# Sliding-window attention, one head to a slot: two complementary triangles merged in PSUM by a predicated copy, exponentiated once, parted on Pool

## Chip, cores, metric

One core of one Trainium2 chip. The metric is the device time in microseconds (us) of one execution. A kernel's time is the median of its runs. The runs e1 to e8 were made on one chip and e9 to e12 on another, each beside before on the same chip. TensorE is called PE, VectorE DVE, ScalarE ACT, GpSimd Pool. "Low clock" means the stretches in which the profile shows PE's granted clock at one half; the clock given for a run is the mean over its span, 1 being full speed.

## The reference, cut to what matters

```python
# A: full attention, B: sliding window; both: S=2048, D=512, H=32 heads of Dh=16
# x, wqkv, wo: bf16, normal * 0.05
scores = einsum("bhqd,bhkd->bhqk", q, k) * (Dh ** -0.5)
# B only, with W = 256:
mask = (idx[:, None] - idx[None, :] >= 0) & (idx[:, None] - idx[None, :] < W)
scores = where(mask, scores, -1e9)
p = softmax(scores);  o = einsum("bhqk,bhkd->bhqd", p, v);  out = o @ wo
# result: concatenate([A, B], axis=-1)
```

In B a block of 128 queries sees three blocks of 128 keys: its *own*, of which it may use the triangle key <= query; the *middle* one, whole; and the *far* one, of which it may use the triangle key > query. The two triangles are complementary: laid over each other they fill one 128x128 block exactly. The change rests on that.

## The kernel before

A *slot* is a PSUM tile of three parts of 512 fp32 columns, called banks here: PE writes scores (keys on the partitions, queries on the columns), ACT takes the exponential of all 1536 columns in one instruction, PE multiplies the result with V some slots later. There are two score buffers, so the scores of slot s+2 can only start when the exponential of slot s is done. Everything else (projections, masks, output) is put in between as fill.

A head has 16 dimensions and a guard row, so its score matmul is issued on 32 rows (32\*128 in the trace, where a matmul over all rows is 128\*128). Four heads of a group sit on four row groups (`tile_position=(32 * jb.j, 0)`). A slot takes three consecutive jobs, so its matmuls use three different row groups. In front of them goes a matmul over all 128 rows whose result is overwritten. It is called the warming matmul because of what it does to the granted clock: without it in window slots the clock was 0.861 in place of before's 0.939 (e3 below).

```python
def scores(self, slot):                     # before
    sps = self.ps.tile([P, SLOT, 512], FP32, name="sps", tag="sps", bufs=2)
    for b, jb in enumerate(slot["jobs"]):
        r = slice(32 * jb.j, 32 * jb.j + KR)
        ...
        if b == 0 and self.filled < 2:      # the warming matmul, full AND window slots
            kT, k0 = self.kT[jb.inst, jb.g // 2, jb.subs[0][0] // 4]
            self.nc.tensor.matmul(sps[:, 0, 0:WARM], lhsT=kT[:, gg, k0:k0 + P],
                                  rhs=qT[:, gg, 0:WARM], start=True, stop=True)
        for kt, q0, q1, o in jb.subs:
            ...
            self.nc.tensor.matmul(sps[:, b, o:o + q1 - q0], lhsT=kT[r, gg, k0:k0 + P],
                                  rhs=qT[r, gg, q0:q1], start=True, stop=True,
                                  tile_position=(32 * jb.j, 0))

# run(), cut: per slot
self.exps(sl)
if s + 2 < len(slots):
    self.scores(slots[s + 2])
self.values(s - 1 - any(j.inst for j in sl["jobs"]))
# ... then fill work
```

A window head of before is 3 x 512 columns: own, middle and far blocks are all exponentiated, then DVE multiplies the own triangles by a mask (`tensor_mul`, line 491) and Pool zeroes the far ones (`affine_select`, line 493).

## Time and profile before

| | before |
|---|---|
| time, median of 4 runs | 1170.76 us (1166.48 to 1172.31) |
| span of the profiled run, mean granted clock | 1169.9 us, 0.939 |
| ACT busy / PE busy | 94% / 79% |
| time at the low clock | 145 us in 21 periods |

The prediction below shows the engines' busy line, the groups and a steady stretch of the timeline. Three more lines matter here. The first is from the page's second part, the granted clock in 40 equal slices, in tenths of full speed; then the largest wait of ACT (who waits <- for whom: us in all, times, longest); then the stretch from 300 to 500 us (PE, PE weight load, DVE, ACT, Pool busy, granted clock, DMA share, GB/s).

```profile
PEclk9999899998999898999999999999999999976777
```
```profile
ACT pT L480 <- PE sps L462: 31.1, 64, 2.1
```

### The profile page before, as it was taken

Reading aid. Unit: us, or ns where it says so; the run is one execution under the profiler, and the core shown is the slowest. Engines: PE = TensorE matmul, PEld = TensorE weight load, DVE = VectorE, ACT = ScalarE, POOL = GpSimd, SP = SyncE. Lnnn points to the kernel's source line nnn. Section 1 sums busy time; section 2 is a strip of 40 time slices with the busy share of each in tenths; the row PEclk is TensorE's granted clock in tenths of the full one; section 3 lists DMA queues with packets and bytes.
Section 4 is the critical chain, followed back from the end, with each engine's and each line's share of the span. In section 5 each row is a group of like instructions: output and inputs, shape, how many; then the busy total and the mean of one; then the engine's idle time right before and its main releaser. Section 6 shows DMA issues by size and latency. Waiting matters only on the chain.

```text
span 1169.9 us, 17451 instructions
## 1 busy us (share of the span) xinstructions
PE 926.1 (79%) x6844; PEld 270.6 (23%) x6944; DVE 298.2 (25%) x674; ACT 1098.6 (94%) x841; POOL 119.0 (10%) x316
## 2 busy tenths in 40 slices
PE   6788888878878887777778787787777887788893
PEld 3222222222222222222222222222222222222221
DVE  3442121132123222222322232224223132320101
ACT  3789999998999999999999999999999999999992
POOL 4000000010001001011200121102112011210100
PEclk9999899998999898999999999999999999976777
DMA  6022421221222112211220221124012112210101
GB/s 207 10 77 75 99 83 41 61 63 52 65 78 76 45 42 65 70 47 61 83 66 32 75 76 54 39 68 118 26 48 65 65 65 69 66 43 18 57 19 55
DMA packets 72810, 73.87 MB, mean 63 GB/s; under 512 B 22688, under 2 KB 55832, under 8 KB 72728
## 3 DMA queue, kind: packets, MB, share of 16 engines
q1 hardware_dynamic: 69656, 68.83, 19.3%
q10 hardware_dynamic: 2432, 1.84, 0.5%
q0 software_dynamic: 640, 2.10, 0.5%
q8 instruction: 54, 0.88, 0.3%
q14 instruction: 28, 0.23, 0.1%
HBM read 39.06 MB, written 31.58 MB: 60 GB/s over the span
## 4 chain that ended last, share of the span: by engine, by line
ACT 62%; PE 21%; issue 11%; DVE 3%; DMA 1%; POOL 0%; ACTq 0%; another core or an unknown queue 0%; SPq 0%; DVEq 0%; POOLq 0%
ACT pT L480 61%; PE sps L462 6%; PE sps L457 6%; PE ms L202 4%; PE op L514 4%; DVE va L285 1%; DVE osb L533 1%; PE ms L591 0%; DMA den<-od 0%; DVE pT L491 0%; DMA rb<-rd 0%; PE sps L358 0%; ACT xT L610 0%; DVE padmax L394 0%; DVE kTa L392 0%
## 5 line engine op out<-in xcount | busy, mean ns | idle before, releaser
L480 ACT ACTIVATE pT<-sps 128x1536 bf16<-128x1536 f32 (+4 forms) x827 | 1088.4, 1566 | 32.8 <-PE sps L462 31.1
L457 PE MATMUL sps<-qTa,kTa 128*128 128x512 bf16 x659 | 261.0, 396 | 159.2 <-ACT pT L480 152.9
L462 PE MATMUL sps<-qTa,kTa 32*128 32x512 bf16 x2048 | 286.5, 404 | 1.5 <-ACT pT L480 1.5
L514 PE MATMUL op<-pT,va 128*32 128x512 bf16 x2048 | 216.4, 412 | 0.5 <-DVE osb L533 0.3
L493 POOL TENSOR_SCALAR_AFFINE_SELECT pT<-pT 128x256 bf16<-128x256 bf16 (+2 forms) x224 | 102.5, 475 | 967.7 <-issue 556.6
L462 PEld LDWEIGHTS <-kTa 32*128 32x128 bf16 x2048 | 68.2, 91 | 395.3 <-issue 395.3
L491 DVE TENSOR_TENSOR pT<-pT,mlo 128x256 bf16<-128x256 bf16 (+2 forms) x256 | 74.9, 334 | 136.3 <-ACT pT L480 134.9
L457 PEld LDWEIGHTS <-kTa 128*128 128x128 bf16 x659 | 64.3, 98 | 144.4 <-issue 124.4
L514 PEld LDWEIGHTS <-va 128*32 128x32 bf16 x2048 | 53.7, 94 | 125.5 <-issue 125.0
L457 PE MATMUL sps<-qTb,kTb 128*128 128x512 bf16 x128 | 51.2, 400 | 34.8 <-ACT pT L480 32.7
L533 DVE COPY osb<-op 128x512 f32<-128x512 f32 x64 | 44.2, 691 | 85.2 <-PE op L514 84.9
L462 PE MATMUL sps<-qTb,kTb 32*128 32x384 bf16 (+2 forms) x704 | 58.4, 289 | 0.0
L220 DVE CAST kst<-ms 128x512 bf16<-128x512 f32 x28 | 19.4, 691 | 141.4 <-PE ms L202 141.4
L343 DVE CAST ob<-ms 128x512 bf16<-128x512 f32 x28 | 19.4, 691 | 131.8 <-PE ms L202 131.8
L301 DVE CAST qs<-ms 128x512 bf16<-128x512 f32 x31 | 21.4, 690 | 115.1 <-PE ms L202 115.1
L514 PE MATMUL op<-pT,vb 128*32 128x384 bf16 (+2 forms) x704 | 36.6, 290 | 0.9 <-DVE osb L533 0.7
L202 PE MATMUL ms<-xT,wq 128*128 128x512 bf16 x91 | 32.2, 408 | 4.7 <-issue 4.3
L462 PEld LDWEIGHTS <-kTb 32*128 32x128 bf16 x704 | 16.9, 93 | 79.7 <-issue 79.7
L202 PE MATMUL ms<-wv,xT 128*128 128x512 bf16 x103 | 32.0, 398 | 4.2 <-issue 1.6
L202 PE MATMUL ms<-xT,wk 128*128 128x512 bf16 x89 | 30.9, 413 | 3.5 <-issue 2.7
L285 DVE CAST vb<-ms 128x512 bf16<-128x512 f32 x16 | 11.1, 692 | 84.5 <-PE ms L202 84.5
L312 DVE CAST gs<-ms 8x512 bf16<-8x512 f32 x31 | 21.0, 677 | 20.0 <-PE ms L310 20.0
(80 smaller groups left out, 274.8 us busy)
## 6 DMA issues: line engine op xcount, KB each, us to landing
od<-osb SPq DMA_DIRECT2D x64, 256.0 KB
oc<-od SPq DMA_DIRECT2D x32, 256.0 KB
rb<-rd SPq DMA_DIRECT2D x32, 256.0 KB
kTb<-kd SPq DMA_DIRECT2D x16, 256.0 KB
qTb<-qd SPq DMA_DIRECT2D x16, 256.0 KB
qd<-qs SPq DMA_DIRECT2D x31, 128.0 KB
qTa<-qd SPq DMA_DIRECT2D x15, 256.0 KB
out_dram<-ob SPq DMA_DIRECT2D x30, 128.0 KB
```

What stands on the lines that cost most here:

```text
L202: self.nc.tensor.matmul(bank, lhsT=lhs(c), rhs=rhs(c), start=(c == 0), stop=(c == NC - 1))
L220: copy(out=kst[:], in_=bank)
L285: copy(out=v3[:, :, 1:VP], in_=bank.rearrange("p (h d) -> p h d", d=DH))
L301: copy(out=qs[:], in_=bank)
L312: self.nc.vector.tensor_copy(out=gs[:], in_=b[0:8, :])
L457: self.nc.tensor.matmul(sps[:, 0, 0:WARM], lhsT=kT[:, gg, k0:k0 + P], rhs=qT[:, gg, 0:WARM], start=True, stop=True)
L462: self.nc.tensor.matmul(sps[:, b, o:o + q1 - q0], lhsT=kT[r, gg, k0:k0 + P], rhs=qT[r, gg, q0:q1], start=True, stop=True, tile_position=(3 ...
L480: nc.scalar.activation(out=pT[:, b:e, :n], in_=sps[:, b:e, :n], func=ACT.Exp, scale=SCALE)
L491: nc.vector.tensor_mul(out=v, in0=v, in1=self.mlo[:, 0:e - b, :])
L493: nc.gpsimd.affine_select(v, v, pattern=[[0, e - b], [-1, P]], compare_op=ALU.is_ge, fill=0.0, base=-1, channel_multiplier=1)
L514: self.nc.tensor.matmul(op[32 * jb.j:32 * jb.j + 32, q0:q1], lhsT=self.v[jb.inst, kt][:, h * VP:h * VP + 32], rhs=slot["pT"][:, b, o:o + q ...
L533: nc.vector.tensor_copy(out=osb[:], in_=self.op[i, p, g][:])
```

## The change

Intent: take exponentials away from ACT, which sets the time. A window slot becomes one head. Its nine score matmuls fill own and middle blocks (1024 columns) and, behind them, the far blocks (512 columns). DVE copies the far triangles over the forbidden halves of the own blocks, PSUM to PSUM, by a predicated copy. ACT then exponentiates 1024 columns in place of 1536, and Pool parts the triangles afterwards.

```diff
 def scores(self, slot):
+    jb = slot["jobs"][0]
+    if i == 1:                                   # a window slot: one head, no warming matmul
+        r = slice(32 * jb.j, 32 * jb.j + KR)
+        for kt, q0, q1, o in jb.near + jb.far:
+            ...
+            self.nc.tensor.matmul(sps[:, o:o + q1 - q0], lhsT=kT[r, gg, k0:k0 + P],
+                                  rhs=qT[r, gg, q0:q1], start=True, stop=True,
+                                  tile_position=(32 * jb.j, 0))
+        m = jb.blocks(sps[:], "merged")
+        ...
+        self.nc.vector.copy_predicated(m, mask.broadcast_to(tuple(m.shape)),
+                                       jb.blocks(sps[:], "last"))
+        return
+    if self.filled < 2:                          # warming matmul: full slots only
         ...
 def exps(self, slot):
+    nc.scalar.activation(out=pT[:, :n], in_=sps[:, :n], func=ACT.Exp, scale=SCALE)
-            for kind, o in jobs[b].blocks:
-                if kind == "d":
-                    nc.vector.tensor_mul(out=v, in0=v, in1=self.mlo[:, 0:e - b, :])
-                else:
-                    nc.gpsimd.affine_select(...)
+            nc.gpsimd.affine_select(jb.blocks(pT[:], "last"), m, ...)   # far triangle out
+            m = jb.blocks(pT[:], "own")
+            nc.gpsimd.affine_select(m, m, ...)                          # own triangle stays
 def slots(self):                                 # heads spread between the full slots
+            for m, h in enumerate(flat):
+                extra.append((a0 + 2.5 + m * (a1 - a0 - 6) / len(flat), h))
 # cut: classes _Job and _Window, values() by groups, smaller rings of buffers
```

## The prediction

> **What bounds the kernel now.** I read the page's first and second parts, then the groups with shapes kept apart, then the timeline around a few slots, then the waits.

> ```profile
> PE 926.1 (79%) x6844; PEld 270.6 (23%) x6944; DVE 298.2 (25%) x674; ACT 1098.6 (94%) x841; POOL 119.0 (10%) x316
> ```
> ScalarE is busy 94% of the span, nearly all of it (1088.4 us on the page) in the exponentials of line 480. PE at 79% comes second and is not far off.

> ```profile
> L480 ACT ACTIVATE pT<-sps 128x1536 bf16<-128x1536 f32 x782 | 1058.6, 1608 | 30.4 <-PE sps L462 28.9 <-DVE pT L491 1.0
> L480 ACT ACTIVATE pT<-sps 128x1024 bf16<-128x1024 f32 x9 | 9.6, 1091 | 0.0
> L480 ACT ACTIVATE pT<-sps 128x768 bf16<-128x768 f32 x10 | 8.6, 918 | 0.0
> ...
> L491 DVE TENSOR_TENSOR pT<-pT,mlo 128x384 bf16<-128x384 bf16 x86 | 30.9, 381 | 77.1 <-ACT pT L480 76.3 <-POOL pT L493 0.7
> ...
> L493 POOL TENSOR_SCALAR_AFFINE_SELECT pT<-pT 128x384 bf16<-128x384 bf16 x70 | 43.2, 625 | 265.7 <-issue 177.9 <-ACT pT L480 79.7 <-POOL pT L493 4.4
> ```
> The mean of 1608 ns is not what an exponential costs: 782 of them in 1058.6 us is 1.35 us each, because neighbours overlap. The masks on VectorE and Pool wait for ScalarE; nothing on ScalarE waits for them but 1.0 us. So taking masks off VectorE is worth nothing by itself.

> ```profile
> 403.98 0.38 PE L457 MATMUL sps<-qTa,kTa 128*128 128x512 bf16 x1 [0.31 <-ACT pT L480]
> 404.28 0.10 PEld L462 LDWEIGHTS <-kTa 32*128 32x128 bf16 x3 [0.59 <-issue]
> 404.29 0.39 PE L462 MATMUL sps<-qTa,kTa 32*128 32x512 bf16 x3
> 404.61 0.10 PEld L514 LDWEIGHTS <-va 128*32 128x32 bf16 x4 [0.23 <-issue]
> 404.61 0.40 PE L514 MATMUL op<-pT,va 128*32 128x512 bf16 x4
> 404.94 0.10 PEld L457 LDWEIGHTS <-kTa 128*128 128x128 bf16 x1 [0.23 <-issue]
> 405.32 0.38 PE L457 MATMUL sps<-qTa,kTa 128*128 128x512 bf16 x1 [0.31 <-ACT pT L480]
> ```
> This is the steady rhythm. PE waits until the exponential of slot s has freed one of the two score buffers, runs a warming matmul, the three score matmuls of slot s+2 at once, and values. The next release comes 1.34 us later: that is the true price of one 1536-column exponential. The scores are complete 0.70 us after the release, so they are ready 0.6 us early.

> **The cost of an exponential.** The trace has exponentials starting 1.330 us apart for 1536 columns and 0.904 us for 1024, which is 0.83 ns a column; taking 1.343 us for 1536 from the matmuls' releases, 1024 cost 0.917, 896 cost 0.810, 512 cost 0.490. The 782 large ones then need 1050.2 us and the 45 small ones 29.3, together 1079.5. From the first exponential's start to the last one's end the trace shows 1121.2 us, so 41.7 us are stalls. About 15 us of idling lie before 100 us (projections of the full instance crowd PE) and about 9 after 1000 us (PE on the lowered clock). In the middle are some 15 stalls of 1.1 to 1.2 us where the granted clock halves for a moment (matmuls of 0.38 us turn into 0.62), and about 9 us at window units with uneven slots.

> [...] A stalled exponential pays more: the one at 1026.29 us, that had waited for PE, took 1.45 us, which is 0.17 over its columns. [...] the three score matmuls of a slot, on three row groups, start 3 ns apart.

> **The change, part by part.** *Removed on ScalarE.* In the built program the list of exponentials has 682 of 1536 columns and one of 1024 (the full instance), 96 of 1024 and 32 of 896 (the window, a head each). That is 682 x 1.343 + 97 x 0.917 + 32 x 0.810 = 915.9 + 88.9 + 25.9 = 1030.8 us, against 1079.5: **48.7 us less** on the path that sets the end, mostly because a head exponentiates 1024 columns in place of 1536.

> *Added ahead of the exponential.* A window slot now holds one head, so its nine score matmuls (1536 columns) all use one row group and run in series; then VectorE merges 4 x 128 columns from PSUM to PSUM; only then may ScalarE start. From the release of the buffer at time 0: 0.03 to PE's start; 1536 columns at 2.4 per ns (512-column projection matmuls start 0.215 us apart) with about 3 ns between matmuls (the startup transposes of 128 columns, each with new weights, are 56 ns apart) = 0.67, and the last one's pipeline 0.16, so 0.86; 0.05 to VectorE (a PE end at 428.62 and its copy at 428.67); the merge, taken as the 0.69 of the 512-column PSUM copy; 0.06 to ScalarE. So the input is ready at 1.69, and the exponential, no longer overlapped, ends 0.17 + 0.85 later, at 2.71. Undisturbed, it would end at 1.343 + 0.917 = 2.26. **A stall of about 0.44 us for each of 96 heads, 42 us.** The 32 heads of the first quarter have six matmuls of 1152 columns and merge 256 (0.42): 0.03 + 0.69 + 0.05 + 0.42 + 0.06 + 0.93 = 2.18 against 2.15, about 1 us in all. VectorE is busy 19% of the time with other things than masks ((298.2 - 74.9) / 1170), half of one being 0.35 us: up to 0.07 us each if waits fall at random, and since many of its operations come before the merge's turn I count 3 us for all 128.

> *Moved.* The 256 mask products (75 us) leave VectorE and 128 merges come (96 x 0.69 + 32 x 0.42 = 80 us): even. Pool gets 256 selects, the most of 512 columns; from 334, 468 and 625 ns for 128, 256 and 384 columns I extrapolate 0.77 us, so about 180 us in place of 104. Window values are now issued after the full unit's, slots later, so this is hidden. Those values come as one burst of 36 matmuls, about 0.75 us of PE: the following slots catch up, and PE has gained some slack since window slots run no warming matmul.

> *Returned.* The uneven window slots of before (about 9 us of stalls) are gone. Startup's filler is 40 x 128 columns in place of 24 x 256 and no longer waits for the padding selector: at most 1 us.

> Sum: 1171 - 48.7 + 42 + 1 + 3 - 9 - 1 = **1158 us**.

> **The rivals.** (1) *The merge is hidden and ScalarE's saving comes through whole*: then 1171 - 48.7 - 5 is about 1117. For it: VectorE is idle 75% of the time, and the merge waits for no other slot. Against it: the 0.6 us of slack that scores have now is smaller than 0.69 + 0.3 of added chain, and two score buffers forbid an earlier start. (2) *The chain is longer than I think*: [...] (3) *The clock.* When ScalarE waits for VectorE, PE waits too[...]. At half clock the window's scores take 1.3 us and its stall grows to about 1.1: with a third of window slots so, +20 us, 1180.

> **Range and chances.** The gain on ScalarE is arithmetic. What I don't know is the chain of 96 slots, where 0.1 us is 10 us of the time; a chain shorter by 0.25 us gives 1134, one longer by 0.3 gives 1187. So 1125 to 1190 eight times in ten. Faster by over 2% needs under 1147.6, a chain about 0.11 us shorter than mine or fewer clock drops: 0.34. Slower needs over 1194.5, rival 2 in full: 0.12. The rest, 0.54, within 2%.

> **What would show it.** The page after should show ScalarE busy near 1050, at a share near 91%, and a wait of its exponentials for VectorE's merge of some 40 us that before doesn't have; merges of 0.69 and 0.42 us; nine window scores spaced as their columns. If that wait is small, rival 1 holds; if merges last 1.2 us, or the nine take over 1 us, rival 2; if the granted clock is lower than 0.939 with window scores of double length, rival 3. I am wrong on the whole if ScalarE stalls somewhere else: at the bursts of window values, or behind VectorE work that waits for a transfer (its reciprocals waited 55.5 us for transfers in all), since the merges now queue behind it.

## More of the kernel before

```profile
300.00:500.00 200.00, 159.98 (x1189) 45.59 (x1207) 52.61 (x121) 194.28 (x159) 17.51 (x44) 0.96 0.20 61
```

Each of the four slices with an 8 holds 6.8 to 10.2 us at half speed. ACT hardly waits: 31 us for PE in the whole kernel, and it is busy 194 of the 200 us.

## The result, and the profile after

| | before | after |
|---|---|---|
| time, median of 4 runs | 1170.76 us | 1254.65 us (1250.15 to 1258.31) |
| ratio to before, 95% interval | | 1.0721 (1.0667 to 1.0775) |
| mean granted clock of the profiled run | 0.939 | 0.817 |
| time at the low clock (periods) | 145 us (21) | 462 us (41) |

A ratio is always the mean time of one kernel's fast runs over that of the other's in the same rounds, so it is not quite the ratio of the medians. Executions over 1.5% slower than the fastest of the same kernel are left out of the means. The change made the kernel 7.2% slower, and the prediction's range does not hold it.

The page's busy line and granted clock:

```profile
PE 1045.6 (83%) x7436; PEld 348.2 (28%) x7536; DVE 308.6 (25%) x545; ACT 1072.0 (85%) x825; POOL 172.0 (14%) x348
...
PEclk8998978679999866977898788869865989676667
```

ACT does less work, as intended, but is busy for only 85% of a longer span. PE is busy 120 us more although its warming matmuls before window slots are gone. The second line says why: many slices have 6, 7 or 8.

Groups of ACT and DVE with shapes kept apart (busy us, mean ns of one | idle just before them, and what ended it):

```profile
L484 ACT ACTIVATE pT<-sps 128x1536 bf16<-128x1536 f32 x682 | 943.5, 1472 | 55.1 <-PE sps L470 52.1
L484 ACT ACTIVATE pB<-sps 128x1024 bf16<-128x1024 f32 x96 | 98.3, 1024 | 82.5 <-DVE sps L456 67.6 <-PE op L523 14.0 <-DVE den L558 0.9
L484 ACT ACTIVATE pB<-sps 128x896 bf16<-128x896 f32 x32 | 29.4, 917 | 9.2 <-DVE sps L456 5.4 <-PE op L523 3.8
```
```profile
L456 DVE COPY_PREDICATED sps<-after,sps 128x512 f32<-128x512 int8 x96 | 66.8, 696 | 262.8 <-PE sps L449 221.1 <-ACT pT L484 28.5 <-issue 12.8
L456 DVE COPY_PREDICATED sps<-after,sps 128x256 f32<-128x256 int8 x32 | 13.7, 429 | 85.2 <-PE sps L449 82.2 <-issue 3.0
```

The shapes and counts are those predicted, and so is the price of a merge. The idle time before window exponentials is 92 us in all, 73 of it for the merge. In the timeline at full clock (start, duration, engine, what, idle before) the chain looks like this:

```profile
443.13 0.82 PE L449 MATMUL sps<-qTb,kTb 32*128 32x256 bf16 x9 [0.25 <-ACT pT L484]
...
444.05 0.70 DVE L456 COPY_PREDICATED sps<-after,sps 128x512 f32<-128x512 int8 x1 [0.43 <-PE sps L449]
...
444.84 1.02 ACT L484 ACTIVATE pB<-sps 128x1024 bf16<-128x1024 f32 x1 [0.42 <-DVE sps L456]
```

Nine matmuls in 0.82 us, 0.10 to DVE, a merge of 0.70, 0.09 to ACT: 1.71 us from PE's start to ACT's. And at half clock:

```profile
489.28 1.45 ACT L484 ACTIVATE pT<-sps 128x1536 bf16<-128x1536 f32 x1 [0.18 <-PE sps L470]
489.66 0.61 PE L462 MATMUL sps<-qTa,kTa 128*128 128x512 bf16 x1
490.20 0.61 PE L470 MATMUL sps<-qTa,kTa 32*128 32x512 bf16 x3
...
491.71 1.46 PE L449 MATMUL sps<-qTb,kTb 32*128 32x256 bf16 x9
...
493.27 0.70 DVE L456 COPY_PREDICATED sps<-after,sps 128x512 f32<-128x512 int8 x1
```

The nine matmuls now take 1.46 us, with one row group of four at work. Between 486 and 491 us full slots follow each other every 1.63 us instead of 1.34, because PE, with its matmuls at 0.61 us, has become the bound there (busy 4.81 of the 5.00 us, ACT 4.44). So a low clock costs in full slots too, which the change never touched. The same stretch as shown of before:

```profile
300.00:500.00 200.00, 167.44 (x1246) 57.33 (x1262) 49.88 (x92) 177.83 (x140) 33.13 (x66) 0.84 0.19 59
```

ACT does 16 us less in these 200 us, at a clock of 0.84 in place of 0.96.

**Where the 87 us come from.** I took each exponential's start-to-start time in the trace, less 50 ns and 0.8333 ns a column, as its stall (a floor fitted to before's trace, where most exponentials of 1536 columns start 1.330 us before the next and most of 1024 columns 0.903), and sorted stalls by the clock just then (own sums over the trace's records):

```
us of stall (number of slots)    full clock    changing      half clock    sum
before, all exponentials         18 (732)      8 (34)        26 (60)        52
after, full slots (1536)         16 (443)      9 (52)        54 (186)       79
after, window slots (1024, 896)  40 (70)       15 (18)       54 (41)       109
```

Stalls grew from 52 to 188 us, by 136. The saving on ACT computed in the prediction is 48.7. The difference, 87 us, is the difference of the two spans (1256.6 - 1169.9).

**What goes with the clock.** The low-clock periods last multiples of 3.41 us, from 3.41 to 27.31 us in before's trace and from 3.41 to 47.79 in after's, but for the last of each, which the end of the span cuts. The granted clock in these records is 1 or one half and nothing between. Long idling of PE does not explain most of the drops: in the 3.41 us before a drop of after, the longest gap between matmuls is 0.64 us in the median. So I weighted every matmul's streaming time in such a stretch of 3.41 us by the share of the array that it uses, taking the largest form in the traces, 128\*128, as the whole (rows/128 x columns/128: 1 for a warming matmul, 1/4 for one score or value matmul). This is my own sum over the matmul records, and the limit of 0.38 is fitted by eye:

```
stretches at full clock:      weight under 0.38: dropped / all    over 0.38: dropped / all
before                          19 / 29                              2 / 271
after                           38 / 60                              3 / 173
e3 (before, less warming)       32 / 37                              0 / 215
e5 (before, narrow warming)     29 / 39                              0 / 218
e10 (three heads, warming)      18 / 24                              1 / 266
```

Over 0.38 the clock hardly ever drops, in any of the fourteen traces (3 of 173 at the most). Under it, it drops about two times in three, so in these traces 0.38 is a level below which it can fall, and not one at which it must. An estimate from the durations shows where the kernels lie. 512 columns are taken as 0.213 us (most 512-column projection matmuls of after start 0.215 us apart or a little more). A full slot streams 0.213 us at weight 1 (warming), 0.213 on three row groups (0.16) and, in three slots of four, 0.213 of values on four column groups (0.16 on average): 0.53 in 1.343 us, or 0.40, to which fill work adds. A window slot of after has only its nine matmuls at a quarter, 0.64 x 1/4 = 0.16, and as much again of values, 0.32 in some 1.49 us (0.917 for the exponential and its median stall of 0.57): 0.21. The trace bears this out. Among after's stretches at full clock from 45 to 1120 us, those without scores of a window slot have a median weight of 0.48, and 12 of 123 end in a drop; those with one window slot have 0.39, and 24 of 85.

### The profile page after: what moved, and what is told of

The parts are those of the page before. It is cut to its first block, busy times and chain, and to the rows that moved or that the text cites. A ratio compares the mean times of both kernels' runs of the same rounds, so it can differ in the third digit from the quotient of the medians.

```text
span 1256.6 us, 18485 instructions
## 1 busy us (share of the span) xinstructions
PE 1045.6 (83%) x7436; PEld 348.2 (28%) x7536; DVE 308.6 (25%) x545; ACT 1072.0 (85%) x825; POOL 172.0 (14%) x348
## 3 DMA queue, kind: packets, MB, share of 16 engines
q1 hardware_dynamic: 69656, 68.83, 17.8%
## 4 chain that ended last, share of the span: by engine, by line
ACT 40%; PE 39%; issue 13%; DVE 6%; DMA 2%; ACTq 0%; another core or an unknown queue 0%; DVEq 0%
ACT pT L484 35%; PE sps L470 8%; PE sps L462 8%; PE sps L449 8%; PE op L523 8%; PE ms L193 6%; ACT pB L484 4%; DVE sps L456 3%; DVE va L276 1%; DMA kTa<-in_A_x_dram 1%; DVE osb L542 1%; DMA xT<-in_B_x_dram 0%; DMA wk<-in_B_wqkv_dram 0%; DVE padmax L385 0%; PE sps L349 0%
## 5 line engine op out<-in xcount | busy, mean ns | idle before, releaser
L484 ACT ACTIVATE pT<-sps 128x1536 bf16<-128x1536 f32 (+1 forms) x683 | 944.4, 1472 | 55.1 <-PE sps L470 52.1
L462 PE MATMUL sps<-qTa,kTa 128*128 128x512 bf16 x659 | 295.3, 448 | 120.2 <-ACT pT L484 90.0
L470 PE MATMUL sps<-qTa,kTa 32*128 32x512 bf16 x2048 | 311.3, 450 | 1.5 <-ACT pT L484 1.5
L491 POOL TENSOR_SCALAR_AFFINE_SELECT pB<-pB 128x512 bf16<-128x512 bf16 (+1 forms) x128 | 74.2, 580 | 980.4 <-ACT pB L484 980.4
L484 ACT ACTIVATE pB<-sps 128x1024 bf16<-128x1024 f32 (+1 forms) x128 | 127.7, 997 | 91.7 <-DVE sps L456 73.0
L456 DVE COPY_PREDICATED sps<-after,sps 128x512 f32<-128x512 int8 (+1 forms) x128 | 80.6, 629 | 348.0 <-PE sps L449 303.4
L449 PE MATMUL sps<-qTb,kTb 32*128 32x128 bf16 (+1 forms) x1056 | 125.3, 271 | 33.4 <-ACT pT L484 30.2
L449 PEld LDWEIGHTS <-kTb 32*128 32x128 bf16 x1056 | 94.0, 107 | 93.6 <-issue 79.9
L462 PEld LDWEIGHTS <-kTa 128*128 128x128 bf16 x659 | 66.9, 102 | 167.0 <-issue 148.0
L496 POOL TENSOR_SCALAR_AFFINE_SELECT pB<-pB 128x512 bf16<-128x512 bf16 x128 | 81.6, 637 | 8.7
L523 PE MATMUL op<-pB,vb 128*32 128x128 bf16 (+1 forms) x1056 | 30.6, 268 | 0.9 <-DVE osb L542 0.9
```

Source lines behind the costliest of these rows:

```text
L449: self.nc.tensor.matmul(sps[:, o:o + q1 - q0], lhsT=kT[r, gg, k0:k0 + P], rhs=qT[r, gg, q0:q1], start=True, stop=True, tile_position=(32 * ...
L456: self.nc.vector.copy_predicated(m, mask.broadcast_to(tuple(m.shape)), jb.blocks(sps[:], "last"))
L462: self.nc.tensor.matmul(sps[:, 0:WARM], lhsT=kT[:, gg, 0:P], rhs=qT[:, gg, 0:WARM], start=True, stop=True)
L470: self.nc.tensor.matmul(sps[:, b * 512:(b + 1) * 512], lhsT=kT[r, g % 2, k0:k0 + P], rhs=self.qT[0, p, g // 2][r, g % 2, :], start=True, s ...
L484: nc.scalar.activation(out=pT[:, :n], in_=sps[:, :n], func=ACT.Exp, scale=SCALE)
L491: nc.gpsimd.affine_select(jb.blocks(pT[:], "last"), m, pattern=z + [[-1, P]], compare_op=ALU.is_ge, fill=0.0, base=-1, channel_multiplier=1)
```

## The experiments

All were timed in three rounds beside before, and all passed the comparison with the reference. Before's median was 1171.16 (e1 to e4), 1170.09 (e5 to e8), 1166.51 (e9 to e11) and 1166.03 (e12).

| run | kernel | median us | ratio to before (95%) | clock |
|---|---|---|---|---|
| | after | 1254.65 | 1.0721 (1.0667 to 1.0775) | 0.817 |
| e1 | after, no merge | 1201.96 | 1.0244 (1.018 to 1.0308) | 0.852 |
| e2 | after, warming before window scores | 1279.5 | 1.0941 (1.0882 to 1.1001) | 0.840 |
| e3 | before, no warming before window scores | 1194.57 | 1.0205 (1.016 to 1.025) | 0.861 |
| e4 | after, merge beside an exponential | 1209.29 | 1.0321 (1.0271 to 1.0372) | 0.868 |
| e5 | before, warming on 32 rows in window slots | 1206.3 | 1.0320 (1.0272 to 1.0367) | 0.866 |
| e6 | after, heads two slots later | 1249.63 | 1.0708 (1.0644 to 1.0771) | 0.821 |
| e7 | e4 and e6 together | 1206.88 | 1.0320 (1.0271 to 1.0369) | 0.844 |
| e8 | e7, warming between the scores | 1236.47 | 1.0498 (1.0394 to 1.0603) | 0.860 |
| e9 | three heads to a window slot, merge beside | 1175.34 | 1.0082 (1.002 to 1.0143) | 0.890 |
| e10 | e9 with warming | 1159.66 | 0.9943 (0.9903 to 0.9983) | 0.930 |
| e11 | e10, heads later | 1165.5 | 0.9983 (0.9917 to 1.005) | 0.916 |
| e12 | e10, merge not beside | 1201.98 | 1.0314 (1.0265 to 1.0363) | 0.906 |

**e1: is it the wait for the merge?** The merge is deleted. The far triangles then carry exponentials of the wrong scores, a wrong result. The comparison does not notice: with inputs of 0.05 x normal, q and k come out near 0.06 and a scaled score near 0.003, so every exponential is nearly 1.

```diff
-            self.nc.vector.copy_predicated(m, mask.broadcast_to(tuple(m.shape)),
-                                           jb.blocks(sps[:], "last"))
```

> The changed kernel without the merge (wrong result on purpose): the exponential of a head waits for its nine score matmuls alone. Theory A (the granted clock follows how much of the array PE used in the last 3.4 us, and the merge's wait thins that use): clock back to 0.90 or more, time 1120 to 1150. Rival B (the merge's chain costs 0.5 us a head and the clock has its own causes): clock stays near 0.82, time 1254 less 128 x 0.5, about 1185 to 1200. Rival C (nine matmuls in one row group are what lowers the clock): clock near 0.82 as well, time above 1185.

Measured 1201.96 us at a clock of 0.852. Not the 1120 to 1150 and the 0.90 of theory A, by which the merge's wait thins the use of PE. The time is just over rival B's 1185 to 1200 and fits rival C, but the clock rose by more than either allowed. The waits of ACT, by who is waited for:

```profile
ACT pT L482 <- PE sps L468: 75.1, 134, 2.2
...
ACT pB L482 <- PE sps L449: 7.8, 19, 1.3
```

Window exponentials no longer wait for much (7.8 us, and 17.0 for a ring of buffers, e6), but full slots wait 75 us for PE, against 52.1 in after and 31.1 in before. So the merge is worth some 55 us at the most, what it does to the clock included, and without it the kernel is still 31 us slower than before with 48.7 us less on ACT. About 80 us are lost to something else, and the granted clock is the line of the page that stands out.

**e2: put the warming matmul back.** If the missing warming matmul is the cause, adding it in front of the nine scores should help.

```diff
         if i == 1:
             r = slice(32 * jb.j, 32 * jb.j + KR)
+            self.nc.tensor.matmul(sps[:, 0:WARM], lhsT=kT[:, gg, k0:k0 + P],
+                                  rhs=qT[:, gg, 0:WARM], start=True, stop=True)
             for kt, q0, q1, o in jb.near + jb.far:
```

> The changed kernel with the warming matmul put in front of the scores of window slots too, as full slots have it and as the kernel before had it. It lengthens each head's chain by 0.3 us, 38 us in all if nothing else moved. Theory A: the clock rises to 0.88 or more, and the time is 10 to 40 us shorter than 1254 in spite of the longer chain. Rival B: the time is 20 to 40 us longer, clock unchanged. Rival C: the same as B.

A miss for theory A: 1279.5 us, 25 slower, which is the time of rivals B and C. The clock did rise (0.84), but the matmul stands at the head of the very chain that ACT waits for:

```profile
ACT pB L488 <- DVE sps L460: 115.5, 119, 2.7
```

The wait for the merge went from 73.0 to 115.5 us. At the head of this chain warming costs more than the higher clock (0.840 against 0.817) wins back.

**e3: take it away from before.** The same question without the chain: before, with the warming matmul in full slots alone.

```diff
-            if b == 0 and self.filled < 2:
+            if b == 0 and self.filled < 2 and jb.inst == 0:
```

> The kernel before with its warming matmul left out in window slots alone (the slots whose first job is of the window); no merge, no serial heads. Theory A: the clock falls from 0.94 to about 0.88 and the time grows by 15 to 40 us. Rivals B and C: no change within 5 us.

A hit for theory A: 1194.57 us, 23 slower than before, at a clock of 0.861, with 127 matmuls *less* in its page and no merge anywhere. The page's clock line:

```profile
PEclk9999999978899888998788998887887998765577
```

**e5: rows or busy time?** Is it that PE idles, or that too little of the array is used? Before again, the window slots' warming matmul kept at its 512 columns but on one row group.

```diff
+                if jb.inst == 0:
                     ... as before
+                else:
+                    self.nc.tensor.matmul(sps[:, 0, 0:WARM], lhsT=kT[r, gg, k0:k0 + P],
+                                          rhs=qT[r, gg, 0:WARM], start=True, stop=True,
+                                          tile_position=(32 * jb.j, 0))
```

> The kernel before with the warming matmul of window slots kept, same 512 columns and the same time on PE, but on 32 of 128 rows in place of all. Theory A' (a 3.4 us window in which columns x rows used x columns used falls under about 0.38 of the full array halves the clock): a quarter of the weight, so nearly as if it were gone: clock 0.86 to 0.89, 1185 to 1198 us. Rival D (what counts is how long PE is busy, whatever the rows): clock 0.94, 1171 us.

A hit on the clock, 0.866, and 8 us over the range in time, 1206.3 us: worth no more than no warming matmul at all (e3: 1194.57, 0.861). The page's clock line:

```profile
PEclk9999899887897887998799978997999989786567
```

The matmul on 32 rows is followed in its row group by the same 512 columns of scores, so in both kernels 1024 columns stream one after the other. The rows are the main difference, but not the only one: the scores of the other two row groups now run beside the narrow matmul in place of behind the wide one, and a window slot's burst, from its first matmul's start to its last one's end, takes 0.59 us in the median, against 0.71 in before and 0.40 in e3. Some 60% of the time that warming adds to PE is thus still there, and almost nothing of its effect on the clock (0.866, against 0.861 in e3 and 0.939 in before). This is the most direct evidence here that the clock follows the part of the array in use and not PE's being occupied. In after, too, the weighted sum tells stretches that drop from those that don't better than streaming time alone does (a random pair is ordered rightly in 97% against 92%; in e5, 98% against 89%). In before, e3 and e9 to e12, where no row group works alone for long, streaming time alone orders them equally well (99% each in before).

**e4: the merge beside an exponential.** Blocks are laid out by bank: own in bank 0, far in bank 1, middle in bank 2. The middle blocks' 512 columns are exponentiated while DVE merges, then the merged 512. The tile framework's dependence between the two, which touch different banks, is taken out; no data is shared.

```diff
+            mms(jb.own + jb.far)
             ... copy_predicated ...
+            for x in mms(jb.mid):
+                self.tc.declare_no_dep(x.ins, slot["merge"].ins, reason="other PSUM bank")
-        nc.scalar.activation(out=pT[:, :n], in_=sps[:, :n], ...)
+        for lo, hi in [(0, n)] if jobs[0].key[0] == 0 else [(1024, n), (0, 512)]:
+            e = nc.scalar.activation(out=pT[:, lo:hi], in_=sps[:, lo:hi], ...)
```

> The changed kernel with a head's blocks laid out by bank: the blocks to be merged first, then the four whole blocks, which are exponentiated (512 columns) while VectorE merges; then the merged ones (512). Two exponentials cost 0.06 us more than one of 1024. Correct result. Theory A and rival B: the stall of 0.5 us a head is gone, ScalarE's floor is 1039 us; A expects clock 0.90 or more and a time of 1125 to 1145, B the old clock and about 1190. Rival C: clock near 0.82, about 1190 or more.

1209.29 us, not 1125 to 1145. The chain did as designed; the timeline of one head:

```profile
436.36 0.82 PE L448 MATMUL sps<-qTb,kTb 32*128 32x128 bf16 x12 [0.25 <-ACT pT L489]
...
437.07 0.70 DVE L458 COPY_PREDICATED sps<-after,sps 128x512 f32<-128x512 int8 x1 [0.21 <-PE sps L448]
437.44 1.19 ACT L489 ACTIVATE pB<-sps 128x512 bf16<-128x512 f32 x2
```

The merge begins before the last scores are done and lies beside the first of two exponentials. The wait for the merge is down to 0.4 us, and 45 us came back. But 318 us of the run are at the low clock, and the stalls of full slots are 96 us (after: 79). As in e1, taking the merge off the path leaves a clock problem behind.

**e6, e7: is it the ring of result buffers?** After shows a third wait: eight window exponentials, 17.8 us in all, wait until PE has read an old result buffer. In e6 the heads come two full slots later, which takes that wait away; e7 does it to e4.

```diff
-                extra.append((a0 + 2.5 + m * (a1 - a0 - 6) / len(flat), h))
+                extra.append((a0 + 4.5 + m * (a1 - a0 - 8) / len(flat), h))
```

> The changed kernel with each unit's first window head 2 slots later, so that the ring of 8 result buffers has been read by then. If the 17.8 us in which exponentials wait for PE to read an old buffer are a cost of their own [...]: 20 to 40 us shorter, 1215 to 1235, and that wait gone. If they only shift: within 8 us of 1254.

> The merge beside an exponential (1209 us, clock 0.868) with the heads 2 slots later. Its exponentials waited 16.4 us for old buffers: 15 to 35 us shorter, 1175 to 1195, clock 0.88 to 0.90.

The wait went, and the time moved by 5 and 2 us, inside the spread of the runs; by the ratios to before it is 1.5 and 0 us. e6 thus came out as its second alternative has it, that the waits only shift, and e7 missed. What ACT no longer waits for the ring it partly waits for the merge, in e6 78.5 us in place of 73.0:

```profile
ACT pB L484 <- DVE sps L456: 78.5, 107, 2.2
```

**e8: warming inside the head.** e7 with a warming matmul on all rows between the merged blocks' scores and the middle blocks', where I thought it would lie beside the merge.

```diff
+            x = self.nc.tensor.matmul(sps[:, 1024:1024 + WARM], lhsT=kT[:, gg, k0:k0 + P],
+                                      rhs=qT[:, gg, 0:WARM], start=True, stop=True)
-            for x in mms(jb.mid):
+            for x in [x] + mms(jb.mid):
```

> As e7, with a full-array warming matmul between the blocks that are merged and the whole blocks, where it lengthens no chain at the full clock. Theory A': it adds 0.21 us of full array to each window slot, so clock 0.91 or more and 1130 to 1160 us, faster than both kernels. Rival (the clock is low for other reasons, the scores of one row group): clock as in e7, and at the low clock the longer PE work makes it 5 to 20 us longer than e7.

A miss: the clock went up from 0.844 to 0.860, and yet e8 was slower than e7, by 21 us by the ratios of the fast runs (the median of 1236.47 us, 30 above e7's, has the two slow ones in it). The middle scores, now exponentiated first, stand behind the warming matmul:

```profile
ACT pB L493 <- PE sps L448: 39.1, 47, 2.1
```

In e7 this wait was 16.7 us in 32 times. Twelve matmuls in one row group take 0.82 us (e4's timeline), and one more among them made this wait 22 us longer: the serial head itself must become shorter.

**e9, e10, e11: three row groups at once.** A window slot now holds the middle blocks of head t, the triangles of queries 0 and 1 of head t+1, and those of queries 2 and 3 of head t+2. Four such slots make the same four heads; the twelve 128-column matmuls run on three row groups. The merge lies beside the middle blocks' exponential. e10 adds the warming matmul, e11 the later heads.

```diff
+        for n, q in ((1, 0), (2, 2)):            # triangles of two other heads
+            ...
+            self.parts.append(((t + n) % GH, own + far))
+        self.parts.append((t, [blk(k0 - 1 + q, q, 1024 + P * a) for a, q in enumerate(qs)]))
...
+            if WARMB and self.filled < 2:        # e9: False, e10 and e11: True
+                self.nc.tensor.matmul(sps[:, 0:WARM], lhsT=kT[:, gg, k0:k0 + P],
+                                      rhs=qT[:, gg, 0:WARM], start=True, stop=True)
+            for n in range(4):
+                for j, subs in jb.parts:         # three row groups in turn
+                    ...
```

> As e4 (merge beside an exponential, no warming matmul in window slots), but a window slot holds the whole blocks of one head and triangles of two others, so that its score matmuls run on three row groups at once and are done in 0.33 us in place of 0.8. Same number of columns, merges and exponentials. Theory A'' (once the clock is low PE is the bound, and nine matmuls in one row group then fill 1.3 us at a quarter of the array, which keeps it low): 1150 to 1185 us, clock 0.88 or more. Rival (it is only the missing warming matmul): within 10 us of e4's 1209, clock near 0.87.

> As e9 with the warming matmul in front of window slots, as in full slots. At the full clock the merged blocks are ready 1.54 us after the release, before the 512-column exponential of the whole blocks ends at 1.83, so nothing waits. ScalarE's floor 1039 us. Theory A'': clock 0.92 or more, 1120 to 1150 us, faster than both kernels. Rival (e8's miss repeats: more PE work in window slots only costs): 1200 or more.

> e10 with the heads 2 slots later, so that no exponential waits for an old result buffer. e6 gained 5 us by that and e7 2 us: 0 to 15 us less than e10.

e9, a hit, with e4's arithmetic on three row groups, took 1175.34 us (the profiled run, clock 0.890, is its fastest; the others had 0.857 to 0.884): 34 less than e4 (28 by the ratios). e10 took 1159.66, another 16 less, at a clock of 0.93, and beats both kernels: 0.6% faster than before (the interval ends at 0.9983) and 95 us faster than after. It was expected at 1120 to 1150, so a part of the saving is still not realised. e11, expected 0 to 15 us below e10, is not faster: a miss. The clock, a window slot and the wait for the merge in e10:

```profile
PEclk9999989899999989999999999989998999786667
```
```profile
431.84 0.38 PE L440 MATMUL sps<-qTb,kTb 128*128 128x512 bf16 x1
432.14 0.23 PEld L450 LDWEIGHTS <-kTb 32*128 32x128 bf16 x12 [0.69 <-issue]
432.15 0.40 PE L450 MATMUL sps<-qTb,kTb 32*128 32x128 bf16 x12
...
433.00 0.62 ACT L487 ACTIVATE pB<-sps 128x512 bf16<-128x512 f32 x1
433.03 0.69 DVE L456 COPY_PREDICATED sps<-after,sps 128x512 f32<-128x512 int8 x1
...
433.75 0.60 ACT L491 ACTIVATE pB<-sps 128x512 bf16<-128x512 f32 x1
```
```profile
ACT pB L491 <- DVE sps L456: 0.8, 3, 0.4
```

Twelve score matmuls take 0.40 us in place of 0.82, so that even behind a warming matmul they end 0.71 us after its start.

**e12: which half?** e10 with the declared independence taken out, so that both exponentials wait for the merge.

```diff
-            self.tc.declare_no_dep(e.ins, slot["merge"].ins, reason="other PSUM bank")
```

> This is e10 with one thing undone: both exponentials of a window slot wait for the merge again, as in the changed kernel; three row groups and the warming matmul stay. What is open is how the 95 us between the changed kernel and e10 divide. Theory A (the serial nine matmuls in one row group are the larger part, through the low clock): in e10's trace the twelve scores are complete 0.72 us after the release, so a merge of 0.69 and two hand-overs of 0.1 put the exponentials at about 1.6 us in place of 1.34: about 0.26 us for each of 96 slots, 25 us over e10, with some us of a lower clock: 1180 to 1200 us, clock 0.89 to 0.92. Rival B (the merge in series is nearly all of the loss): near the changed kernel, 1230 us or more, clock under 0.86. Rival C (the merge in series costs nothing once the scores are early): within 6 us of e10, 1155 to 1166.

1201.98 us at 0.906, just over the 1180 to 1200 of theory A and far from B and C. One head in the timeline, and the wait:

```profile
436.49 0.38 PE L440 MATMUL sps<-qTb,kTb 128*128 128x512 bf16 x1 [0.31 <-ACT pT L485]
436.80 0.40 PE L450 MATMUL sps<-qTb,kTb 32*128 32x128 bf16 x12
437.31 0.70 DVE L456 COPY_PREDICATED sps<-after,sps 128x512 f32<-128x512 int8 x1 [2.80 <-PE sps L450]
...
438.10 0.60 ACT L487 ACTIVATE pB<-sps 128x512 bf16<-128x512 f32 x1 [0.32 <-DVE sps L456]
```
```profile
ACT pB L487 <- DVE sps L456: 40.6, 94, 1.6
```

With e12 the two parts of the loss stand in a square, in ratios to before:

| ratio (clock) | merge ahead of the exponentials | merge beside one |
|---|---|---|
| one row group, no warming | after 1.0721 (0.817) | e4 1.0321 (0.868) |
| three row groups, warming | e12 1.0314 (0.906) | e10 0.9943 (0.930) |

Taking the merge off the path is worth 4.0 and 3.7 hundredths, some 45 us; going from one row group without warming to three with it is worth 4.1 and 3.8, some 46 us. That second step changes three things at once: the rows in use, the warming, and the length of the score chain, which matters where the merge is ahead (the wait for the merge is 73.0 us in after, 40.6 in e12). Beside an exponential, e9 splits it: 2.4 for the three row groups and 1.4 for the warming. The two steps add up, and neither is "the larger part", as theory A had it.

## Why the prediction was wrong

Point by point, by its own steps:

- **Removed on ACT: right.** The counts are exact, and the stalls' sum above closes with its 48.7 us.
- **The price of a merge: right.** 0.696 and 0.429 us against 0.69 (before's 512-column copies from PSUM take 691 ns) and 0.42, an estimate. Rival 2, the longer chain (merges of 1.2 us, which was the author's estimate and not taken from a trace, or nine matmuls of over 1 us at full clock), is refuted: 0.70 and 0.82 us.
- **The chain at full clock: right in mechanism, a little small.** The recorded sum has a slip: its terms add up to 1.66 us from the release and not 1.69, as the 0.03 before PE's start is counted twice (likewise in the 2.18 of the small heads); that is 3 us of the time. Its 0.16 for the end of the last matmul fits the trace: most 512-column projection matmuls are recorded with 0.38 or 0.39 us and start 0.215 to 0.227 apart. From PE's start to ACT's start they make 1.63 us, and 1.71 was measured: the hand-overs are 0.10 and 0.09, not 0.05 and 0.06. (The copy from which the 0.05 was read starts at 428.98, after a PE end at 428.93; the times in the text are not in the trace, the difference is.) The median stall of the 48 large heads at full clock is 0.57 us against 0.44, their mean 0.715. At full clock the window slots stall 40 us where the prediction's terms give 48 x 0.44 + 22 x 0.03 = 22, so 18 us more. About 8 of these are not the chain: five of the eight waits for the ring of result buffers fall here, 9.9 us of stall where the terms give 1.8.
- **Moved work: right.** DVE is even (308.6 against 298.2 us of before), Pool hides its selects (no wait for them in after's list of waits), at 637 ns for 512 columns rather than the extrapolated 0.77 us. The burst of 36 value matmuls takes 0.85 us in the median, where the prediction estimates 0.75.
- **Returned, 9 us for uneven window slots: 5 too much,** as before's stalls of such slots come to 4.4 us by the floor used above.
- **The step that failed is rival 3, "+20 us, 1180", and its being left out of the sum.** Its picture of one event was good: 1.46 us for window scores at half clock (1.3 predicted), a median stall of 1.38 (1.1), and 36 of the 97 exponentials of 1024 columns (one of them not the window's) at half clock, "a third". Three things were wrong. It counted only window slots, but the low clock lies on 186 full slots as well, whose stalls grew from 48 to 79 us: at half clock PE sets their rhythm. It took the low clock for a consequence of PE waiting for DVE, whereas e3 gets a clock of 0.861 with no merge at all, and deleting the merge (e1) brings the clock from 0.817 to 0.852 only, with 0.939 in before. Nor does before's page tie the low clock to an idle PE: at 6 to 7 tenths of the clock, PE is busy for 8 or 9 tenths in four of the last five slices. And the text booked the missing warming matmul as slack gained for PE ("PE has gained some slack since window slots run no warming matmul"), although e3 shows that without it the clock falls (0.939 to 0.861).

The predicted change in stalls is 42 + 1 + 3 - 9 - 1 = +36 us; measured it is +136. Of the 100 us between, 18 are window slots at full clock (the chain, and five waits for the ring) and 5 the uneven slots. The other 77 are stalls of slots at low or changing clock, some 31 in full slots and some 46 in window slots, which the sum did not have. The eight waits for the ring of buffers lie among the window's stalls, and e6 shows that they were not worth their 17.8 us.

**What stays open.** When the clock comes back is not settled. At half clock, stretches that stay low have a median weight of 0.58 in after and those that recover 0.68, but the two overlap, and near the end of the kernels stretches of 0.70 stay low. The experiments varied the rows in use and not the columns: that a value matmul on 32 columns counts a quarter is an assumption that fits. The smaller rings and the bursts of window values were not undone one by one; e10 has them all and is no slower than before. And e10 is not followed to the end: ACT's exponentials cost about 43 us less there than before (48.7 less some 6 for 128 additional instructions at 50 ns), and only 7 us of that show in the time. By the sum of stalls used above, its exponentials stall 81 us against before's 52; some 11 of the 29 more are waits for the ring, and e11, which takes them away, is no faster.

## What to carry to other kernels

When a change takes work off the engine that sets the time, ask what it does to how much of PE's array is used in every stretch of some 3.4 us, and not only how long PE is busy: here the clock fell almost only where under about 0.38 of the array was streaming, and a fallen clock slows slots that the change never touched (the stalls of full slots went from 48 to 79 us). Matmuls of few rows should sit on different row groups at the same time; put in series on one they cost twice here, as a longer chain (0.82 us for twelve in e4, 0.40 in e10) and as a lower clock (0.868 in e4, 0.890 in e9). An engine inserted between PE and ACT belongs beside a part of the exponentials (worth some 45 us here), and a warming matmul only where the scores are early (it cost 25 us at the head of a tight chain, and won 16 where there was room).
